# A fused attention and MLP kernel: w_out loaded in 2 KB rows, w_in read in plain slices, and the first tile transposed in fp32

## The chip, the cores and the metric

The kernel runs on one core of a Trainium2 chip. The metric is the device time of one execution in microseconds; the kernel before takes 257.83 us (median of 3 runs, 257.62 to 258.07).

The engines are called PE (TensorE: matmuls and transposes), ACT (ScalarE: exp, tanh, copies), DVE (VectorE), POOL (GpSimd) and SP (SyncE, which only issues DMAs here). PEld is the loading of PE's stationary operand, which runs beside the matmuls. SPq and POOLq are DMA issues of those engines.

## The reference

The computation is an attention over 4 batches of 8 heads, 768 positions, head size 64, followed by an MLP over the 3,072 tokens of 512 features:

```python
scores = q @ k.T / 8                      # per batch and head, 768 x 768
# retrieval heads: causal mask; the others: causal and
# (one of the first 4 keys, or among the last 64 keys)
scores = where(mask, scores, -1e9)
a = softmax(scores)
x = (a @ v), heads laid side by side      # 3072 x 512
h = x @ w_in                              # 512 x 2048
g = h - tanh(h)
out = g @ w_out                           # 2048 x 512
```

Inputs and output are fp32. Which heads are retrieval heads comes as data.

## The kernel before

The tokens are cut into 12 tiles of 256 (three per batch). For each tile the kernel loads q, k and v in fp32, casts them to fp16, transposes q and k, computes scores, exp, the product with v, transposes the result x, and runs the MLP on it: `ph` = w_in times x, `th` = tanh, `gt` = ph - tanh, `po` = gt times w_out. In tiles 0 to 2 PE transposes q and k (`st_T`); in later tiles the heads are sorted by rank, and the DMA engines transpose.

No engine's program is written in order. Operations are collected with a duration, their reads and writes; a list scheduler, run while the program is built, plays them through and emits them in the order of its clock. So a changed duration can move instructions anywhere:

```python
class Plan:
    def op(self, eng, ns, fn, r=(), w=(), dma=None, prio=None, port=False, after=None): ...
    def run(self):
        ...                                   # the earliest operation that is ready goes next
        if dma:
            packets, each = dma               # packets, ns of each on one of 16 DMA engines
            rings["POOL" if e == "POOL" else "SP"].append(
                [i, t + ns + (1200 if e == "POOL" else 300), each, packets * each / 16]
            )
        ...
        for i in order:
            self.ops[i][2]()
```

Tokens are loaded by SP, a block of 128 positions at a time. A row of one head is 256 bytes:

```python
op("SP", max(420, 128 * nh * 1.1),
   lambda: nc.sync.dma_start(
       out=r()[:, i, h0 : h0 + nh, :],
       in_=src[b, h0 : h0 + nh, s0 : s0 + 128, :].rearrange("h p d -> p h d")),
   w=[("raw", idx, i, x) ...], dma=(128 * nh, 18.3), after=after)
```

The weights are loaded by POOL, which casts them to fp16 on the way. Each w_out load brings 512 rows. Partition p takes four rows that follow each other in memory, 8 KB in one piece:

```python
def load_w_out(j, w_after):
    w = lazy(w_pool, [128, 4, DM], FP16, f"wout{j}", f"wout{j}")
    op("POOL", 900,
       lambda: nc.gpsimd.dma_start(
           out=w()[:].rearrange("p i m -> p (i m)"),
           in_=moe_w_out[j * 512 : (j + 1) * 512, :].rearrange("(p i) m -> p (i m)", p=128)),
       r=w_after, w=[("wout", j)], dma=(512, 77.0))
```

With that layout, row 4p + i of w_out stands in slot i of partition p. So `H_unit` has to produce the features of a block in that order, and takes every fourth column of w_in as the stationary operand:

```python
for cb in range(HP):
    nc.tensor.matmul(
        out=ph()[:, j, :], lhsT=w()[:, cb, c0 + fb % 4 : c0 + 512 : 4],
        rhs=xTs[t]()[:, cb, :], start=(cb == 0), stop=(cb == HP - 1))
```

The first tile is cast by ACT and DVE, and then transposed like tiles 1 and 2:

```python
cast_qk(0, (("ACT", "ACT"), ("ACT", "DVE")), (0,))
load(1, halves=range(2))
for n in (0, 1):                          # n counts pairs of heads
    st_T(n, "ACT", ("DVE", "DVE"))
    for f in scores(n): f()
cast_v(0, ("POOL", "POOL"), (0,))
cast_qk(0, (("ACT", "ACT"), ("ACT", "DVE")), (1,))
...

def st_T(n, eq="DVE", ek=("DVE", "DVE")):
    tp, key = bank([128, 2, 8, 128], FP16, "sc", f"tp{n}")
    ...
    nc.tensor.transpose(out=o, in_=t16s[nm, t]()[:, i, 2*hp : 2*hp+2, :], identity=ident16[:])
    ...                                   # eq copies q out of PSUM, ek[0] and ek[1] copy k
```

The product with v of a pair of heads (`av`) reads the cast values `v`, and for keys far from the query `vf`, a copy scaled by the head's flag.

Of the kernel before, what the change touches and what calls it, by code (L numbers as in the profile page):

```python
# [7 lines left out]
FP32 = mybir.dt.float32  # L8
FP16 = mybir.dt.float16
# [3 lines left out]
TT = 256  # L13
# [136 lines left out]
def kernel(  # L150
# [63 lines left out]
    ones = const.tile([128, 128], FP16, name="ones")  # L214
    warm = const.tile([128, 1], FP32, name="warm")
    ident16 = const.tile([128, 128], FP16, name="ident16")
    A4 = const.tile([128, 4, 128], FP16, name="A4")
    sinks = const.tile([128, 128], FP16, name="sinks")
    nz = const.tile([128, 2 * H], FP32, name="nz")
# [29 lines left out]
    def program(first):  # L249
# [27 lines left out]

        raws = {}

        def paired(nm, t):  # L280

            return nm != "v" and t < 0

        def load(t, names="qkv", halves=(None,), blocks=range(NB), after=None):

            b, g = divmod(t, NG)
            for half in halves:
                h0, nh = (0, H) if half is None else (half * HH, HH)
                for nm in names:
                    src = {"q": q, "k": k, "v": v}[nm]  # L290
                    if (nm, t) not in raws:
                        idx = rot["raw"] = rot.get("raw", -1) + 1
                        raws[nm, t] = (
                            lazy(raw_pool, [128, NB, H, D], FP32, "raw", f"raw_{nm}{t}"), idx
                        )
                    r, idx = raws[nm, t]
                    if paired(nm, t):
                        if blocks[0]:
                            continue
                        op(  # L300
                            "SP", max(420, 128 * nh * 1.1),
                            lambda r=r, src=src, h0=h0, nh=nh: nc.sync.dma_start(
                                out=r()[:].rearrange("p i h d -> p (i h d)").rearrange(
                                    "p (h c) -> p h c", h=H
                                )[:, h0 : h0 + nh, :],
                                in_=src[b, h0 : h0 + nh, g * TT : (g + 1) * TT, :].rearrange(
                                    "h (p e) d -> p h (e d)", e=NB
                                ),
                            ),
                            w=[  # L310
                                ("raw", idx, i, x)
                                for i in range(NB) for x in (range(2) if half is None else (half,))
                            ],
                            dma=(128 * nh, 26.0), after=after,
                        )
                        continue
                    for i in blocks:
                        s0 = g * TT + i * 128
                        op(
                            "SP", max(420, 128 * nh * 1.1),  # L320
                            lambda r=r, i=i, src=src, s0=s0, h0=h0, nh=nh: nc.sync.dma_start(
                                out=r()[:, i, h0 : h0 + nh, :],
                                in_=src[b, h0 : h0 + nh, s0 : s0 + 128, :].rearrange("h p d -> p h d"),
                            ),
                            w=[("raw", idx, i, x) for x in (range(2) if half is None else (half,))],
                            dma=(128 * nh, 18.3), after=after,
                        )

        W_IN = ((0, 512), (512, 512), (1024, 512), (1536, 512))

        def load_w_in(c0, n, w_after):
            w = lazy(w_pool, [128, HP, n], FP16, f"win{c0}", f"win{c0}")
            op(
                "POOL", 900,
                lambda: nc.gpsimd.dma_start(
                    out=w()[:],
                    in_=moe_w_in[:, c0 : c0 + n].rearrange("(cb p) f -> p cb f", p=128),
                ),  # L340
                r=w_after, w=[("win", j) for j in range(c0 // 512, (c0 + n) // 512)],
                dma=(512 * n // 512, {512: 85.0, 1024: 80.0, 2048: 77.0}[n]),
            )
            for j in range(c0, c0 + n, 512):
                w_in_t.append((w, j - c0))

        def load_w_out(j, w_after):
            w = lazy(w_pool, [128, 4, DM], FP16, f"wout{j}", f"wout{j}")
            op(
                "POOL", 900,  # L350
                lambda: nc.gpsimd.dma_start(
                    out=w()[:].rearrange("p i m -> p (i m)"),
                    in_=moe_w_out[j * 512 : (j + 1) * 512, :].rearrange("(p i) m -> p (i m)", p=128),
                ),
                r=w_after, w=[("wout", j)], dma=(512, 77.0),
            )
            w_out_t.append(w)

# [23 lines left out]
        if first:  # L382
# [27 lines left out]
                )  # L410


            select(ident16[:], ones[:], 0.0, 0, 1, -1, "ident", ALU.is_equal)
            select(A4[:, 2, :], ones[:], 0.5, window_i - 1, -1, 1, "A4")
            select(sinks[:], ones[:], 0.5, n_sink_i - 1, 0, -1, "sinks")
# [195 lines left out]
        def t16_keys(nm, t, half):  # L611
            return [("t16q", t, half) if nm == "q" else ("k16", t % 2, half)]

        def cast_qk(t, engines, halves=range(2)):

            for half in halves:
                for nm, es in zip("qk", engines):
                    if (nm, t) not in t16s:
                        t16s[nm, t] = tokens(nm, t)
                    c = t16s[nm, t]  # L620
                    r, slot = raws[nm, t]
                    hs = slice(half * HH, half * HH + HH)
                    cast_op(
                        es[half], NB * HH * D,
                        lambda nm=nm, c=c, hs=hs: (
                            c()[:, :, hs, :].rearrange("p i h d -> p h i d") if paired(nm, t)
                            else c()[:, :, hs, :]
                        ),
                        lambda nm=nm, r=r, hs=hs: (
                            r()[:].rearrange("p i h d -> p (i h d)").rearrange(  # L630
                                "p (h i d) -> p h i d", h=H, i=NB
                            )[:, hs, :, :] if paired(nm, t) else r()[:, :, hs, :]
                        ),
                        r=[("raw", slot, i, half) for i in range(NB)], w=t16_keys(nm, t, half),
                    )

# [181 lines left out]
        def st_T(n, eq="DVE", ek=("DVE", "DVE")):  # L818
            t, hp = divmod(n, HP)
            b, g = divmod(t, NG)  # L820
            tp, key = bank([128, 2, 8, 128], FP16, "sc", f"tp{n}")
            keys = [(*key, x) for x in range(2)]
            if hp == 0:
                qT[t] = lazy(qt_pool, [128, HP, TT], FP16, "qT", f"qT{t}")

            def turn(x, nm):
                for i in range(NB):
                    o = tp()[:, x, i, :]
                    if paired(nm, t):
                        o = tp()[:, x, 0:NB, :].rearrange("p i c -> p (i c)")[:, i : NB * 128 : NB]  # L830
                    nc.tensor.transpose(
                        out=o, in_=t16s[nm, t]()[:, i, 2 * hp : 2 * hp + 2, :], identity=ident16[:],
                    )

            for x, nm in enumerate("qk"):
                op(
                    "PE", 112, lambda x=x, nm=nm: turn(x, nm),
                    r=t16_keys(nm, t, hp * 2 // HP) + ["ident"], w=keys[x : x + 1],
                )

            cost = {"ACT": 373, "DVE": 288}
            kk = kz[b % 2][:, 2 * hp : 2 * hp + 2, :]
            op(
                eq, cost[eq],
# [289 lines left out]
        def H_unit(t, u):  # L1134
# [3 lines left out]
            for j in range(FU):  # L1138

                def mm(j=j):  # L1140
                    fb = u * FU + j
                    w, c0 = w_in_t[fb // 4]
                    for cb in range(HP):
                        nc.tensor.matmul(  # L1144
                            out=ph()[:, j, :], lhsT=w()[:, cb, c0 + fb % 4 : c0 + 512 : 4],
                            rhs=xTs[t]()[:, cb, :], start=(cb == 0), stop=(cb == HP - 1),
                        )

                op(
                    "PE", 4 * 109, mm,  # L1150
                    r=[("win", u * FU // 4)] + x_keys(t), w=[key],
                )
# [106 lines left out]

        for b in range(2):  # L1260
            ones_v(b)
        cast_qk(0, (("ACT", "ACT"), ("ACT", "DVE")), (0,))
        load(1, halves=range(2))
        for n in (0, 1):
            st_T(n, "ACT", ("DVE", "DVE"))
            for f in scores(n):
                f()
        cast_v(0, ("POOL", "POOL"), (0,))
        cast_qk(0, (("ACT", "ACT"), ("ACT", "DVE")), (1,))
        for n in (0, 1):  # L1270
            st_A(n, 0)
            st_A(n, 1)
# [10 lines left out]
            cast_qk(1, (("ACT", "ACT"), ("ACT", "ACT")), (half,))  # L1283
            cast_v(1, ("POOL", "POOL"), (half,))
        if first:
            for c0, n in W_IN:
                load_w_in(c0, n, [("v1", 0, 1, 0)])
        load(2)
        scale_v(0, "POOL")
        scale_v(1)  # L1290
# [136 lines left out]
```

## Time and profile before

| | |
|---|---|
| time, median of 3 | 257.83 us |
| span of the profiled execution | 256.3 us |
| busy PE / PEld / DVE / ACT / POOL | 231.5 / 176.8 / 145.1 / 147.3 / 96.0 us |
| read from and written to HBM | 27.27 and 6.29 MB |
| matmuls of ph, 768 of 256 columns | 100.1 us, 273 ns each |
| matmuls of po, 368 of 512 columns and 32 of 256 | 99.1 us, 373 ns each |
| loads of w_in slices as stationary operand | 113 ns each |
| w_in and w_out, four loads each, issue to landing | 11.2 and 11.0 us (median) |

The duration of one matmul includes the time in PE's pipeline, so matmuls overlap and the mean says nothing of the pace; the distance between starts does. The duration of a DMA from issue to landing includes its time in the queue. A wait in the profile is put down to what ended last. The digit rows of the page cut the span into 40 slices of 6.4 us; each digit is a share in tenths.

The part up to about 50 us is the start: tokens of the first tiles and both weights come in, and attention runs ahead of the MLP. Behind it PE alternates between attention of a later tile and the MLP of an earlier one.

### The profile page before, as it was taken

The page shows a single profiled execution, that of the slowest core. Times are in us where ns is not written, and L with a number is a line of the kernel's source. Part 1 is how long each engine was busy: PE and PEld are TensorE (multiplying, and loading weights), DVE is VectorE, ACT ScalarE, POOL GpSimd, SP SyncE. Part 2 cuts the span into 40 slices and gives each one's busy share as a digit, 9 for nine tenths or more (in the row PEclk, how much of TensorE's full clock was granted, in tenths as well). Part 3 has the DMA queues.
Part 4 walks back from the last instruction along what each step waited for, and adds up shares of the span by engine and source line. Part 5 has one row for each costly group of instructions (what it writes and reads, how often), then busy time and mean ns, then how long its engine had stood idle before and what let it go on. Part 6 is the DMA issues. An engine that isn't in the chain of part 4 may idle for free. (4 is left out here: it accounts for less than half of the span.)

```text
span 256.3 us, 6128 instructions
## 1 busy us (share of the span) xinstructions
PE 231.5 (90%) x2220; PEld 176.8 (69%) x2220; DVE 145.1 (57%) x359; ACT 147.3 (57%) x229; POOL 96.0 (37%) x288
## 2 busy tenths in 40 slices
PE   1788986697899899999979999999999999999992
PEld 0456965485677678777757777777788777777761
DVE  7556768246357764656746545566767554643410
ACT  3578857277364938655556664755666656444330
POOL 5382610139954733928625168318520000000000
PEclk9999999599999999999999999999999999999999
DMA  6999999995699799979999899699970311031121
GB/s 140 218 213 196 209 225 220 220 210 97 154 180 172 144 168 243 185 193 208 161 209 203 168 206 211 164 158 218 200 164 3 83 43 42 3 82 43 41 82 48
DMA packets 120131, 39.25 MB, mean 153 GB/s; under 512 B 114336, under 2 KB 116640, under 8 KB 120096
## 3 DMA queue, kind: packets, MB, share of 16 engines
q1 hardware_dynamic: 117120, 34.49, 69.1%
q0 software_dynamic: 2688, 4.19, 8.9%
q8 instruction: 18, 0.29, 0.5%
q14 instruction: 17, 0.14, 0.2%
q10 hardware_dynamic: 288, 0.14, 0.2%
HBM read 27.27 MB, written 6.29 MB: 131 GB/s over the span
## 5 line engine op out<-in xcount | busy, mean ns | idle before, releaser
L1144 PE MATMUL ph<-xT,win 128*128 128x256 f16 x768 | 100.1, 273 | 0.4 <-DVE gt L1164 0.3
L1203 PE MATMUL po<-wout,gt 128*128 128x512 f16 (+1 forms) x400 | 99.1, 373 | 0.9 <-ACT ot L1179 0.9
L1164 DVE SCALAR_TENSOR_TENSOR gt<-th,ph 128x512 f16<-128x512 f32 x96 | 65.9, 686 | 52.0 <-ACT th L1157 51.6
L1157 ACT ACTIVATE th<-ph 128x512 f32<-128x512 f32 x96 | 57.5, 599 | 59.1 <-PE ph L1144 58.9
L1144 PEld LDWEIGHTS <-win 128*128 128x128 f16 x768 | 80.9, 113 | 8.0 <-issue 0.6
L990 ACT ACTIVATE pt<-sc 128x768 f16<-128x768 f32 (+1 forms) x60 | 54.1, 917 | 23.1 <-PE sc L972 23.0
L1203 PEld LDWEIGHTS <-gt 128*128 128x128 f16 x400 | 37.0, 98 | 23.5 <-issue 1.7
L972 PE MATMUL sc<-qT,kz 128*128 128x256 f16 (+1 forms) x280 | 34.2, 257 | 2.7 <-DMA qT<-t_q 2.1
L1039 PEld LDWEIGHTS <-pt 128*128 128x128 f16 x552 | 27.2, 99 | 13.1 <-issue 4.5
L972 PEld LDWEIGHTS <-kz 128*128 128x128 f16 x280 | 24.1, 102 | 12.6 <-issue 1.8
L669 POOL CAST k<-raw_k 128x128 f16 x72 | 19.4, 316 | 33.3 <-DMA raw_k<-in_k_dram 28.6
L1039 PE MATMUL av<-v,pt 128*128 128x65 f16 x304 | 26.7, 196 | 4.4 <-POOL v L602 4.4
L669 POOL CAST t_q<-raw_q 128x128 f16 x72 | 19.8, 314 | 14.2 <-DMA raw_q<-in_q_dram 8.8
L669 POOL CAST v<-raw_v 128x128 f16 x72 | 19.3, 319 | 11.0 <-DMA raw_v<-in_v_dram 11.0
L1069 DVE TENSOR_TENSOR x16t<-av,rinv 128x128 f32 x72 | 20.9, 290 | 2.1
L1039 PE MATMUL av<-vf,pt 128*128 128x65 f16 x248 | 20.5, 195 | 0.0
L915 ACT ACTIVATE pt<-sc 128x1024 f16<-128x1024 f32 (+1 forms) x18 | 17.2, 956 | 3.8 <-PE sc L901 3.1
L1008 DVE TENSOR_TENSOR pt<-pt,m 128x1024 f16<-128x1024 f16 x16 | 13.5, 842 | 10.0 <-ACT pt L990 10.0
L1179 ACT ACTIVATE ot<-po 128x512 f32<-128x512 f32 (+1 forms) x24 | 14.2, 593 | 8.5 <-PE po L1203 8.5
L1059 DVE RECIPROCAL rinv<-av 128x4 f32<-128x4 f32 x48 | 8.6, 179 | 17.5 <-PE av L1039 17.4
L932 DVE TENSOR_TENSOR pt<-pt,mS 128x512 f16<-128x512 f16 x24 | 9.7, 444 | 7.9 <-ACT pt L915 7.9
L901 PE MATMUL sc<-qT,kz 128*128 128x128 f16 x132 | 10.3, 219 | 0.3 <-ACT pt L990 0.3
(71 smaller groups left out, 122.8 us busy)
## 6 DMA issues: line engine op xcount, KB each, us to landing
out_dram<-ot SPq DMA_DIRECT2D x23, 256.0 KB, 2.2
raw_q<-in_q_dram SPq DMA_DIRECT2D x20, 256.0 KB, 4.2
raw_k<-in_k_dram SPq DMA_DIRECT2D x20, 256.0 KB, 4.3
raw_v<-in_v_dram SPq DMA_DIRECT2D x20, 256.0 KB, 4.7
win<-in_moe_w_in_dram POOLq DMA_DIRECT2D x4, 512.0 KB, 11.2
wout<-in_moe_w_out_dram POOLq DMA_DIRECT2D x4, 512.0 KB, 11.0
raw_q<-in_q_dram SPq DMA_DIRECT2D x8, 128.0 KB, 3.7
raw_k<-in_k_dram SPq DMA_DIRECT2D x8, 128.0 KB, 3.8
```

Of the source, the lines that this page charges most:

```text
L669: nc.gpsimd.tensor_copy(out=o, in_=r()[:, :, at, :])
L915: lambda: nc.scalar.activation(out=pt()[:, :, 0:wid], in_=sc()[:, :, 0:wid], func=AF.Exp, scale=inv_sqrt_d),
L972: nc.tensor.matmul(out=sc()[:, hh, o : o + nb * 128], lhsT=kk[:, hh, jb * KS : jb * KS + 128], rhs=q_of(t, hp)[:, q0 * 128 : (q0 + nb) * 128],
L990: lambda: nc.scalar.activation(out=pt()[:, :, 512 * gi : 512 * gi + wid], in_=sc()[:, :, 0:wid], func=AF.Exp, scale=inv_sqrt_d,),
L1008: nc.vector.tensor_mul(out=pv, in0=pv, in1=m4[:, hs, 256:512].unsqueeze(2).to_broadcast([128, 2, 2, 256]),)
L1039: nc.tensor.matmul(out=av()[:, i, hh, :], lhsT=pt()[:, hh, co : co + 128], rhs=vv, start=(jb == first_jb), stop=(jb == qb),)
L1069: nc.vector.tensor_mul(out=x16s[t]()[:, :, at, :], in0=av()[:, :, hh : hh + 1, 0:D], in1=rinv()[:, :, hh : hh + 1].unsqueeze(3).to_broadca ...
L1144: nc.tensor.matmul(out=ph()[:, j, :], lhsT=w()[:, cb, c0 + fb % 4 : c0 + 512 : 4], rhs=xTs[t]()[:, cb, :], start=(cb == 0), stop=(cb == HP ...
L1157: lambda: nc.scalar.activation(out=th()[:], in_=ph()[:], func=AF.Tanh, scale=1.0 / XS),
L1164: lambda: nc.vector.scalar_tensor_tensor(out=gts[t]()[:, u * FU : (u + 1) * FU, :], in0=th()[:], scalar=-XS, in1=ph()[:], op0=ALU.mult, op ...
L1179: nc.scalar.activation(out=ot()[:, c0:c1], in_=po()[:, c0:c1], func=AF.Copy, scale=1.0 / XS)
L1203: nc.tensor.matmul(out=po()[:, c0:c1], lhsT=gts[t]()[:, f, ts * 128 : ts * 128 + 128], rhs=w_out_t[f // 4]()[:, f % 4, c0:c1], start=(f == ...
```

## The change

Three things are changed by hand.

- w_out comes in single rows of 2 KB: row p of each group of 128 goes to partition p. That is the plain layout, so the slices of w_in that make the stationary operand are 128 columns that follow each other.
- The first tile's q and k are no longer cast. PE transposes the fp32 values as they were loaded, with an fp32 identity and into an fp32 PSUM tile; the copies out of PSUM give fp16.
- Leftovers go: an unused way to load pairs of positions, and a list of column ranges for w_in.

The durations that the scheduler is told for these operations change with them, so the order on every engine is planned anew. The diff, cut to its core:

```diff
+    ident32 = const.tile([128, 128], FP32, name="ident32")
...
-                lambda: nc.gpsimd.dma_start(
-                    out=w()[:].rearrange("p i m -> p (i m)"),
-                    in_=moe_w_out[j * 512 : (j + 1) * 512, :].rearrange("(p i) m -> p (i m)", p=128),
+                lambda: nc.gpsimd.dma_start(
+                    out=w()[:],
+                    in_=moe_w_out[j * 512 : (j + 1) * 512, :].rearrange("(fb p) m -> p fb m", p=128),
                 ),
-                r=w_after, w=[("wout", j)], dma=(512, 77.0),
+                r=w_after, w=[("wout", j)], dma=(512, 85.0),
...
+            select(ident32[:], ones[:], 0.0, 0, 1, -1, "ident32", ALU.is_equal)
             select(ident16[:], ones[:], 0.0, 0, 1, -1, "ident", ALU.is_equal)
...
-            tp, key = bank([128, 2, 8, 128], FP16, "sc", f"tp{n}")
+            dt, ident, ns = (FP32, ident32, 440) if t == 0 else (FP16, ident16, 112)
+            tp, key = bank([128, 2, 16 // mybir.dt.size(dt), 128], dt, "sc", f"tp{n}")
...
+                if t == 0:
+                    c, slot = raws[nm, t]
+                    r = [("raw", slot, i, hp * 2 // HP) for i in range(NB)] + ["ident32"]
+                else:
+                    c, r = t16s[nm, t], t16_keys(nm, t, hp * 2 // HP) + ["ident"]
+                op("PE", ns, lambda x=x, c=c: turn(x, c), r=r, w=keys[x : x + 1])
...
-            cost = {"ACT": 373, "DVE": 288}
+            cost = {"ACT": 373, "DVE": 420 if t == 0 else 288}
...
-                            out=ph()[:, j, :], lhsT=w()[:, cb, c0 + fb % 4 : c0 + 512 : 4],
+                            out=ph()[:, j, :], lhsT=w_in_t[fb // 4]()[:, cb, f0 : f0 + 128],
...
-        cast_qk(0, (("ACT", "ACT"), ("ACT", "DVE")), (0,))
         load(1, halves=range(2))
...
-        cast_qk(0, (("ACT", "ACT"), ("ACT", "DVE")), (1,))
```

More of the change, by code (lines that the diff above doesn't have):

```diff
@@ L278, in program @@
         raws = {}
-        def paired(nm, t):
-            return nm != "v" and t < 0
         def load(t, names="qkv", halves=(None,), blocks=range(NB), after=None):
@@ L296, in load @@
                     r, idx = raws[nm, t]
[L297 to L316, printed above, removed]
                     for i in blocks:
@@ L327, in load, with load_w_in @@
                         )
-        W_IN = ((0, 512), (512, 512), (1024, 512), (1536, 512))
-        def load_w_in(c0, n, w_after):
-            w = lazy(w_pool, [128, HP, n], FP16, f"win{c0}", f"win{c0}")
+        def load_w_in(j, w_after):
+            w = lazy(w_pool, [128, HP, 512], FP16, f"win{j}", f"win{j}")
             op(
@@ L338, in load_w_in @@
                     out=w()[:],
-                    in_=moe_w_in[:, c0 : c0 + n].rearrange("(cb p) f -> p cb f", p=128),
+                    in_=moe_w_in[:, j * 512 : (j + 1) * 512].rearrange("(cb p) f -> p cb f", p=128),
                 ),
-                r=w_after, w=[("win", j) for j in range(c0 // 512, (c0 + n) // 512)],
-                dma=(512 * n // 512, {512: 85.0, 1024: 80.0, 2048: 77.0}[n]),
-            )
-            for j in range(c0, c0 + n, 512):
-                w_in_t.append((w, j - c0))
+                r=w_after, w=[("win", j)], dma=(512, 85.0),
+            )
+            w_in_t.append(w)
         def load_w_out(j, w_after):
@@ L623, in cast_qk @@
                     cast_op(
[L624 to L633, printed above, removed]
+                        es[half], NB * HH * D, lambda c=c, hs=hs: c()[:, :, hs, :],
+                        lambda r=r, hs=hs: r()[:, :, hs, :],
                         r=[("raw", slot, i, half) for i in range(NB)], w=t16_keys(nm, t, half),
@@ L824, in st_T, with turn @@
                 qT[t] = lazy(qt_pool, [128, HP, TT], FP16, "qT", f"qT{t}")
-            def turn(x, nm):
+            def turn(x, c):
                 for i in range(NB):
-                    o = tp()[:, x, i, :]
-                    if paired(nm, t):
-                        o = tp()[:, x, 0:NB, :].rearrange("p i c -> p (i c)")[:, i : NB * 128 : NB]
                     nc.tensor.transpose(
-                        out=o, in_=t16s[nm, t]()[:, i, 2 * hp : 2 * hp + 2, :], identity=ident16[:],
+                        out=tp()[:, x, i, :], in_=c()[:, i, 2 * hp : 2 * hp + 2, :],
+                        identity=ident[:],
                     )
             for x, nm in enumerate("qk"):
[L836 to L839, printed above, removed]
-            cost = {"ACT": 373, "DVE": 288}
+                if t == 0:
[5 more added lines that the diff above has]
+            cost = {"ACT": 373, "DVE": 420 if t == 0 else 288}
             kk = kz[b % 2][:, 2 * hp : 2 * hp + 2, :]
@@ L1141, in mm @@
                     fb = u * FU + j
-                    w, c0 = w_in_t[fb // 4]
+                    f0 = (fb % 4) * 128
                     for cb in range(HP):
                         nc.tensor.matmul(
-                            out=ph()[:, j, :], lhsT=w()[:, cb, c0 + fb % 4 : c0 + 512 : 4],
+                            out=ph()[:, j, :], lhsT=w_in_t[fb // 4]()[:, cb, f0 : f0 + 128],
                             rhs=xTs[t]()[:, cb, :], start=(cb == 0), stop=(cb == HP - 1),
@@ L1285, in program @@
         if first:
-            for c0, n in W_IN:
-                load_w_in(c0, n, [("v1", 0, 1, 0)])
+            for j in range(4):
+                load_w_in(j, [("v1", 0, 1, 0)])
         load(2)
```

## The prediction

> **What bounds the kernel now.** I read the page's busy times and slices first, then the waits, then the busy times by stage, then the timeline around the one long wait, and last the DMA queues of two stretches.
>
> ```profile
> PE 231.5 (90%) x2220; PEld 176.8 (69%) x2220; DVE 145.1 (57%) x359; ACT 147.3 (57%) x229; POOL 96.0 (37%) x288
> PE   1788986697899899999979999999999999999992
> PEclk9999999599999999999999999999999999999999
> DMA  6999999995699799979999899699970311031121
> ```
>
> TensorE (PE) is busy for 90% of the span, and its lows, the tail apart, are in the first ten slices of 6.4 us. The clock digit falls once, to 5, in the eighth slice (44.9 to 51.3 us). The DMA engines are full from the second slice to the ninth.
>
> A busy PE need not be at its pace, so I take the pace from a steady stretch:
>
> ```profile
> 102.09 1.04 PE L1144 MATMUL ph<-xT,win 128*128 128x256 f16 x8
> 102.96 1.03 PE L1203 MATMUL po<-wout,gt 128*128 128x512 f16 x4
> 103.82 0.38 PE L972 MATMUL sc<-qT,kz 128*128 128x256 f16 x3
> ```
>
> Eight matmuls of 256 columns start 0.87 us before the next group: 109 ns each. Four of 512 columns take 0.86 us: 215 ns each. Both are 2.4 columns per ns plus 2 or 3 ns. By that rate all matmuls are about 220 us of streaming; the other 36 us are lost, and I add them up from the start times: 17 us by 42.4, another 6.5 by 52, about 7 between 52 and 160, hardly any until 250, and the 5 us tail. So 42 to 52 is the stage to look at.
>
> ```profile
> PE av L1039 <- POOL v L602: 4.4, 1, 4.4
> POOL v L602 <- DMA raw_v<-in_v_dram: 16.6, 4, 10.9
> ```
>
> These are the waits (total us, times, longest us). By stage:
>
> ```profile
> 24.00:42.40 18.40, 17.16 (x197) 15.58 (x197) 12.68 (x31) 13.95 (x24) 5.06 (x9) 1.00 1.16 214
> 42.40:47.00 4.60, 0.24 (x7) 0.15 (x6) 2.28 (x13) 0.70 (x2) 0.71 (x2) 0.78 1.03 216
> 47.00:52.00 5.00, 5.00 (x37) 3.46 (x37) 1.95 (x8) 1.73 (x2) 0.47 (x1) 0.52 0.99 214
> 52.00:60.00 8.00, 8.00 (x96) 6.21 (x95) 3.82 (x10) 6.45 (x12) 4.28 (x16) 1.00 0.88 192
> ```
>
> The columns are span, busy time of PE, PEld, DVE, ACT and POOL, clock, DMA share, GB/s. PE stands still for 4.36 us, and then runs 5.0 us at a clock of 0.52, which costs another 5.0 x 0.48 = 2.4 us.
>
> ```profile
> 24.80 8.01 SPq L321 DMA_DIRECT2D raw_v<-in_v_dram  x2
> 29.62 2.25 POOL L351 DMA_DIRECT2D wout<-in_moe_w_out_dram x4
> 46.29 1.18 POOL L602 CAST v<-raw_v 128x512 f16<-128x512 f32 x2 [10.88 <-DMA raw_v<-in_v_dram]
> 46.96 0.22 PE L1039 MATMUL av<-v,pt 128*128 128x65 f16 x1 [4.36 <-POOL v L602]
> ```
>
> PE waits for a cast, the cast for the second block of V of tile 2. The landing times give that block an issue at 29.3 and a landing at 46.17 us, 16.9 us later, where the first block landed at 34.9. What it shared the DMA engines with is w_out, whose four parts landed from 37.6 to 45.6. The queues in 25 to 30 us (while w_in is loaded) and in 36 to 40 us (w_out) show how (packets, MB, share of 16 engines):
>
> ```profile
> q0 software_dynamic: 782, 0.78, 91.9%
> q1 hardware_dynamic: 784, 0.20, 29.9%
> ```
>
> ```profile
> q0 software_dynamic: 211, 0.78, 96.7%
> q1 hardware_dynamic: 205, 0.05, 9.7%
> ```
>
> The weights (q0) and the rows of q, k, v (q1, 256 B each) alternate one packet for one. A round takes 5.0 us x 16 / 782 = 102 ns with w_in's 2 KB rows, and 4.0 us x 16 / 211 = 303 ns with w_out's 8 KB rows. So the layout of w_out sets how fast V arrives.
>
> **What the Trainium skill says.** "DMA: Bandwidth & Descriptors", section "Queues, rings and completion order", says that each DMA engine goes round-robin over the queues it has work for, a packet at a time; the counts 782 to 784 and 211 to 205 agree. "TensorE: Matmul & The Clock Gate", Part 1, says that the clock is halved once an activity window of about 3.4 us passes idle; the 0.52 behind the 4.36 us wait agrees, and the waits of 1.8 and 1.7 us later leave the clock at 1.00. The same page, "Terms", gives the array a transpose mode that is 4 times faster for fp32; no fp32 matmul is in this trace, so I leave open whether the new transposes run in one pass or in four.
>
> **The change part by part.**
>
> 1. *w_out in 2 KB rows.* The block of V is 1,024 rows and 16 closing packets: 65 rounds per DMA engine. Before: w_out has (128 + 16) x 4 / 16 = 36 rounds of 303 ns = 10.9 us, with 36 of the 65 rows in them; the other 29 rows follow at about 15 ns, so some 11.3 us. From 33.1 us (the first block's landing less 1.8) that gives 44.4, plus 1.8 to land = 46.2, as measured. After: 65 rounds of 102 ns = 6.6 us, so a landing at 41.5 to 42, a cast of 0.62 us, and a release of PE at about **42.5** in place of 46.96. w_out itself takes (512 + 16) x 4 / 16 = 132 rounds of 102 ns = 13.5 us in place of 10.9. Its last part lands near 48.2; its first user stands 7.4 us of matmuls behind the wait, at 49.9 or later, so this stays hidden. The tokens behind it (q, k, v of tile 3) land some 1.4 us later.
>
> 2. *Plain stationary slices of w_in.* The loads with a step of four elements take 113 ns, those of scores 102 and of po 98. All lie beside matmuls that start every 109 ns, which is the streaming rate: 0.
>
> 3. *First tile in fp32.* Removed: 3 casts on ScalarE of 0.62 us and one on VectorE of 0.43. Added: one select on GpSimd (0.29), wider copies out of PSUM on VectorE (two per head pair, 0.29 each before; the kernel's own plan has 0.42), and dearer transposes: 16 of them. In one pass they cost what the fp16 ones do. In four passes they are 512 columns in place of 128: 160 ns more each at full clock (2.6 us in all), about 320 at half clock (5.1). In this stage the matmuls of 128 columns start 105 to 110 ns apart, so the clock is the low one until about 14 us. The chain of the first pair gains: its q and k land at 4.8 and 6.0 us, and the first exp starts at 8.9; without the casts I get about 8.1 even in four passes. Later pairs give that back. By the end of tile 0 I take the two as even. From 22 us on PE is paced by w_in, whose four parts land at 22.6, 25.9, 29.3 and 32.7 in both.
>
> 4. *The order.* The instructions are ordered by the kernel's own plan, whose costs changed. In the new PE order the eight matmuls of ph of tile 1, unit 3 stand behind the wait for V, no longer ahead of it: 8 x 109 = 0.87 us of work moves behind. PE then comes to the wait near 41.5, so about 1 us of waiting is left, too short to lower the clock. The scores of tile 4 come 3.2 us of PE work earlier, those of tile 5 1.3, of tile 7 1.5.
>
> The sum: 42.5 - 46.96 = -4.5; the work moved behind +0.9; no half clock -2.4: together **-6.0**. Against it: the transposed q of tile 4 landed at 79.7 and was used at 82.6, 2.9 us of slack for 3.2 (+0.3); that of tile 5 at 96.0 for 96.7 (+0.6); tile 7 already waits 1.7 us and comes 1.5 earlier (up to +1.5). **+2.2** in all. -3.8 from 257.8 gives **254.1 us**.
>
> **The rivals.**
>
> - *The start becomes the bound.* If the fp32 transposes take four passes at half clock and their 5.1 us fall on the chain of the head pairs, PE comes to the wait at 44 to 45 instead of 41.5. For it: the chain from transpose to exp is serial there. Against it: w_in paces PE from 22.6 to 33, and the casts leave the chain. Time: 256 to 257.
> - *The gain is given back in tiles 3 to 7.* Loads are tied to PE's progress, but a DMA engine full from 90 to 110 us (share 1.08 and 1.21) may not be able to run 5 us earlier. For it: tile 7's wait on a DMA transpose. Against it: the DMA digits of 5, 6 and 7 between 58 and 115 us, room of several us. Time: 256.5 to 258.
> - *V does not come earlier*, because the share goes by bytes and not by packets. Then w_out's longer stay only costs: about 259. The packet counts speak against it.
> - *More comes of it*: a start earlier by a microsecond and none of the later waits growing: 251.5 to 252.5.
>
> **Range and chances.** The gain at the wait is the surest part (5 to 6 us); what of it survives to the end is not. I put the middle at 254.1, and the range from 251.6 (nearly all kept) to 257.4 (start or middle eats nearly all). Faster by over 2% means under 252.7: 0.23. Slower by over 2% means over 263, which needs a new wait of 5 us on top of no gain: 0.03. Within 2%: 0.74.
>
> **What would show it.** In the new profile: q0 and q1 one for one at about 102 ns a round until about 47 us; V's second block landing near 42; PE's wait for the cast of v at 1 us or less, and no digit of 5 in the clock row; the last w_out landing near 48 with no wait of po on it; the first exp near 8 us; matmul pace of ph still 109 ns. It would be wrong if fp32 transposes of 400 ns or more show PE arriving late at the wait, if the clock falls elsewhere, or if waits on transposed q in tiles 4 to 7 add up to more than about 4 us.

## The result and the profile after

The kernel after takes **0.9848** of the time of the kernel before (95% interval 0.982 to 0.9877): 253.7 and 253.9 us against a median of 257.73 us. Two further timed runs of it, at 257.7 and 259.0 us, were disturbed and are not in the ratio. That is within 2%, and 254.1 us was predicted. The total is right by luck; two of the terms behind it are not, and they nearly cancel.

The page of the kernel after, the busy times first, then the rows of the slices:

```profile
PE 230.2 (91%) x2220; PEld 167.6 (67%) x2220; DVE 144.2 (57%) x358; ACT 144.8 (57%) x226; POOL 97.7 (39%) x289
...
PE   2888986899999899999899899998999999999992
...
PEclk9999999999999999999999999999999999999999
DMA  6999999999899999898999979499960311031111
```

A slice is 6.3 us here. The 5 in the clock row is gone. Of PE's lows around the wait a 6 stays in the seventh slice (37.8 to 44.1 us); single 8s follow in the slices that start at 44, 63, 101, 120, 139 and 170 us. PE's waits (total us, times, longest us):

```profile
PE av L1005 <- POOL v L574: 2.8, 1, 2.8
PE ph L1110 <- DMA xT<-x16t: 2.6, 3, 1.4
```

The wait for V has shrunk from 4.4 to 2.8 us, not to the 1 us that was computed. A new entry stands behind it: PE waits 2.6 us, in three pieces, for transposed x. By stage (span, busy PE, PEld, DVE, ACT, POOL, clock, DMA share, GB/s):

```profile
41.98:44.76 2.78, 0.00 (x1) 0.00 (x0) 1.33 (x11) 0.45 (x1) 0.67 (x2) 1.00 1.23 198
44.76:52.00 7.24, 7.16 (x94) 5.73 (x94) 4.99 (x17) 5.01 (x8) 2.72 (x9) 1.00 1.04 216
```

PE stands still for 2.78 us and goes on at full clock. The timeline around it (start, us, engine, line, operation):

```profile
24.81 8.01 SPq L298 DMA_DIRECT2D raw_v<-in_v_dram  x2
30.32 3.04 POOL L322 DMA_DIRECT2D wout<-in_moe_w_out_dram  x4
44.09 1.18 POOL L574 CAST v<-raw_v 128x512 f16<-128x512 f32 x2 [8.64 <-DMA raw_v<-in_v_dram]
44.76 0.19 PE L1005 MATMUL av<-v,pt 128*128 128x65 f16 x1 [2.78 <-POOL v L574]
```

The V block landed at 43.97 us, where 41.5 to 42 was computed and 46.17 was measured before. The DMA queues tell why. First 34.5 to 36 us, then 40 to 44 us (packets, MB, share of 16 engines):

```profile
q0 software_dynamic: 298, 0.30, 122.3%
q1 hardware_dynamic: 3, 0.00, 0.2%
```

```profile
q0 software_dynamic: 629, 0.63, 92.0%
q1 hardware_dynamic: 625, 0.16, 29.7%
```

In the second stretch the queues alternate one for one, 4.0 x 16 / 629 = 102 ns a round, as computed. In the first the queue of the token rows has three packets in 1.5 us: the block was issued at 29.3, but its packets began only at 36.0 and were at their pace from 36.2. 36.2 plus 65 rounds of 102 ns is 42.9, and the landing came 1.1 us behind.

For all kernels I add up PE's lost time as the prediction did for the kernel before: distance between starts, less columns / 2.4 ns and 2.5 ns. An fp32 transpose counts as 128 columns, so its longer run is in the loss.

| profiled run | wait for V, us | lost by 60 us | lost from 60 to 180 us | lost from 75 to 180 us | waits for DMA in 75 to 180 us | ratio to before |
|---|---|---|---|---|---|---|
| before | 4.4 | 23.7 | 6.6 | 3.9 | 2.1 | 1 |
| after | 2.8 | 20.3 | 6.0 | 5.2 | 3.4 | 0.985 |
| before, 2 KB rows (e1) | 2.1 | 19.0 | 6.8 | 5.9 | 3.8 | 0.990 |
| after, fp16 tile (e8) | 2.4 | 19.0 | 7.1 | 6.5 | 4.2 | 0.989 |
| after, told of V (e5) | 0 | 19.5 | 8.0 | 6.8 | 4.7 | 0.985 |
| before, told of V (e6) | 0 | 17.9 | 8.4 | 8.0 | 4.6 | 0.979 |
| after, V on a second queue (e7) | 0 | 18.2 | 9.1 | 7.4 | 5.6 | 0.993 |
| fp16 tile, told of V (e11) | 0 | 17.7 | 7.5 | 7.4 | 5.5 | 0.987 |
| fp16 tile, told of V and xT (e9) | 0 | 17.9 | 2.8 | 2.7 | none listed | 0.974 |
| before, told of V and xT (e10) | 0 | 17.9 | 3.6 | 3.6 | none listed | 0.976 |
| after, told of V and xT (e12) | 0 | 18.4 | 3.1 | 1.7 | none listed | 0.970 |

The names in brackets are those of the experiments below. The losses are of one profiled execution each, and the ratios come from the timed runs. The profiled execution of e5 took 255.3 us where its four runs span 251.7 to 255.3, that of e6 253.9 where they span 251.0 to 253.9. From 75 to 180 us the first eight kernels lose what they wait for DMA and about 2 us more; e6 has another 1.7 for a halved clock.

### The profile page after: what moved, and what is told of

It reads as the page before. It is cut to its first block, busy times and chain, and to the rows that moved or that the text cites. A ratio compares the mean times of both kernels' runs of the same rounds, so it can differ in the third digit from the quotient of the medians.

```text
span 252.0 us, 6126 instructions
## 1 busy us (share of the span) xinstructions
PE 230.2 (91%) x2220; PEld 167.6 (67%) x2220; DVE 144.2 (57%) x358; ACT 144.8 (57%) x226; POOL 97.7 (39%) x289
## 5 line engine op out<-in xcount | busy, mean ns | idle before, releaser
L1169 PE MATMUL po<-wout,gt 128*128 128x512 f16 (+1 forms) x400 | 98.1, 370 | 1.2 <-ACT ot L1145 1.2
L1110 PEld LDWEIGHTS <-win 128*128 128x128 f16 x768 | 71.4, 98 | 18.6 <-DMA xT<-x16t 3.8
L1005 PEld LDWEIGHTS <-pt 128*128 128x128 f16 x552 | 26.8, 98 | 14.7 <-issue 4.7
L938 PEld LDWEIGHTS <-kz 128*128 128x128 f16 x280 | 23.2, 98 | 11.0 <-DVE kz L780 3.9
L633 POOL CAST t_q<-raw_q 128x128 f16 x72 | 20.3, 317 | 18.4 <-DMA raw_q<-in_q_dram 17.4
L974 DVE TENSOR_TENSOR pt<-pt,m 128x1024 f16<-128x1024 f16 x16 | 11.4, 710 | 8.0 <-ACT pt L956 8.0
```

The costliest lines, as they stand in the source:

```text
L633: nc.gpsimd.tensor_copy(out=o, in_=r()[:, :, at, :])
L938: nc.tensor.matmul(out=sc()[:, hh, o : o + nb * 128], lhsT=kk[:, hh, jb * KS : jb * KS + 128], rhs=q_of(t, hp)[:, q0 * 128 : (q0 + nb) * 128],
L974: nc.vector.tensor_mul(out=pv, in0=pv, in1=m4[:, hs, 256:512].unsqueeze(2).to_broadcast([128, 2, 2, 256]),)
L1005: nc.tensor.matmul(out=av()[:, i, hh, :], lhsT=pt()[:, hh, co : co + 128], rhs=vv, start=(jb == first_jb), stop=(jb == qb),)
L1110: nc.tensor.matmul(out=ph()[:, j, :], lhsT=w_in_t[fb // 4]()[:, cb, f0 : f0 + 128], rhs=xTs[t]()[:, cb, :], start=(cb == 0), stop=(cb == H ...
L1169: nc.tensor.matmul(out=po()[:, c0:c1], lhsT=gts[t]()[:, f, ts * 128 : ts * 128 + 128], rhs=w_out_t[f // 4]()[:, f % 4, c0:c1], start=(f == ...
```

## The experiments

The first four ran beside a kernel before of 257.81 us, the second four beside 256.81, the third three beside 256.41, the last beside 256.92; so ratios are compared, not microseconds.

**e1: only the layout.** The kernel before, its order kept, with w_out in 2 KB rows. The rows of w_out sit in other slots than the features that meet them, so another product is computed; the work is the same.

```diff
-                    out=w()[:].rearrange("p i m -> p (i m)"),
-                    in_=moe_w_out[j * 512 : (j + 1) * 512, :].rearrange("(p i) m -> p (i m)", p=128),
+                    out=w()[:],
+                    in_=moe_w_out[j * 512 : (j + 1) * 512, :].rearrange("(fb p) m -> p fb m", p=128),
```

> The kernel before with w_out loaded in 2 KB rows and nothing else; every engine keeps its order. Theory A (the packet share of w_out sets when V of tile 2 arrives, and that is the gain): V's second block lands near 44.0 instead of 46.2 us, PE is released near 44.8 and has waited 2.3 us instead of 4.4, the clock does not fall, time 253.0 to 254.0 us. Rival B (the gain is the fp32 first tile or the new order): V may land earlier, but the time stays at 257 to 258 us. Rival C (the plain stationary slices of w_in): also 257 to 258, as the slices keep their step of four here.

Measured: 0.990 (0.9871 to 0.9929). V landed at 43.79 us and PE's wait was

```profile
PE av L1039 <- POOL v L602: 2.1, 1, 2.1
```

with the clock at 1.00. The layout alone takes 4.7 us off the lost time by 60 us, and about two thirds of the time that the whole change brings (1.0% of 1.5%, with intervals that overlap a little).

**e2: the change without the layout.** The kernel after with 8 KB rows, the diff of e1 backwards; again another product.

> The changed kernel with w_out in 8 KB rows again, order kept, plain slices kept. Theory A: V's second block lands at 46.2 us, PE waits about 5 us from 42.0, the clock falls to a half for some 4 to 5 us, time 258.0 to 258.8 us. Rivals B and C (fp32 tile, order or plain slices carry the gain): 253.5 to 254.5 us.

Measured: 1.0184 (1.0125 to 1.0243), so slower than before.

```profile
PE av L1005 <- POOL v L574: 4.9, 1, 4.9
```

V landed at 46.37 us, and the clock was half from 44.3 to 51.1. With e1 this settles that the rows of w_out set when V lands. It is slower than was expected, too. The order of the kernel after comes to the wait earlier with less work done, which costs 0.8 us by 60 us; and a wait of 2.56 us for xT at 123.4 halved the clock again, from 126.2 to 129.7, about 1.7 us more.

**e3: only the fp32 tile.** The kernel before with the first tile transposed in fp32 and planned anew; 8 KB rows and stepped slices stay.

```diff
+            dt, ident, ns = (FP32, ident32, 440) if t == 0 else (FP16, ident16, 112)
...
-        cast_qk(0, (("ACT", "ACT"), ("ACT", "DVE")), (0,))
-        cast_qk(0, (("ACT", "ACT"), ("ACT", "DVE")), (1,))
```

> The kernel before with the first tile transposed in fp32 and not cast, planned anew; w_out in 8 KB rows and the stepped slices of w_in as before. Theory A: worth nothing, because PE then waits for V at 46.2 us anyway: 257.3 to 258.5 us, with a wait of 4 to 5 us and one fall of the clock. Rival B: 253.5 to 255 us.

Measured: 0.9982 (0.9958 to 1.0007). The wait was 4.2 us and the clock fell from 48.3 to 51.7. With V late, the fp32 tile and the order that comes with it bring nothing. The new order isn't neutral: it issued the V block at 31.3 us in place of 29.3, and V landed at 47.83.

**e4: the wait without the halved clock.** The kernel before, with the first four products of the ninth pair repeated 16 times ahead of the wait, about 2 us of extra work; the last pass gives the result.

```diff
-                    for jb in range(first_jb, qb + 1):
+                    again = 16 if n == 8 and i == 0 and hh == 0 else 0
+                    for x, jb in [(0, j) for j in range(4)] * again + [
+                        (1, j) for j in range(first_jb, qb + 1)
+                    ]:
```

> The kernel before; the first four matmuls of the product with v on which PE then waits are done 16 times more, 64 matmuls of 65 columns, about 1.9 us of work ahead of the wait, with no use. V arrives as before (PE released at 46.9 to 47.0 us); the wait is 2.4 to 2.6 us instead of 4.4. If the half clock behind the wait is a cost of its own, made by the length of the idle time: the clock stays at 1.00 and the time falls by 2.0 to 2.4 us to 255.3 to 255.7 us. If the clock fell for another reason or costs nothing: 257.5 to 258 us.

Measured: 1.0206 (1.0113 to 1.0299), a miss. The wait was 2.66 us, and the clock fell all the same, from 47.1 to 50.5, and again from 125.6 to 129.0 behind a wait of 2.78 us for xT. These are the two lows of its clock row:

```profile
PEclk9999999799999999999899999999999999999999
```

It doesn't separate wait and clock. What it shows is that a wait of this length may or may not cost the clock: 2.78 us in the kernel after did not. The last section works out which does.

**e5: the same kernel, told when V comes.** In the kernel after the plan believes that the V block lands at 38.3 us. One number changes, and with it only the order: 3.2 us more PE work stands ahead of the wait.

```diff
-                            dma=(128 * nh, 18.3), after=after,
+                            dma=(1750 if (nm, t, i) == ("v", 2, 1) else 128 * nh, 18.3), after=after,
```

> The kernel after, with one number of the kernel's own plan changed: the second block of V of tile 2 counts as 1,750 packets in place of 1,024, so that the plan no longer believes it lands at 38.3 us. Nothing but the order of instructions changes; by the instruction order 28.75 us of matmuls stand ahead of the first product with that V, against 25.58. Theory A (what is left of the gain is the 2.8 us wait that the late V leaves, and PE has other work to put there): PE comes to the wait about 3.2 us later, near 45, the wait is 0 to 0.4 us, the clock stays at 1.00 and the whole takes 2 to 2.8 us less than the kernel after: about 249.5 us of span, 251 to 251.8 us of time, a ratio of 0.973 to 0.978 to the kernel before. Rival B (the gain is given back later, by the transposed q of tiles 4 to 7): the wait goes and waits of 1 us or more appear between 80 and 180 us, the time stays at 253 to 254. Rival C (the work that is moved ahead is itself not ready, tanh or w_out missing): lost time by 60 us stays at 20 us.

Measured: 0.9846 (0.9777 to 0.9916), no different from the kernel after. The wait for V is gone, but waits for xT and qT between 75 and 180 us grew from 3.4 to 4.7 us. Rival C of the expectation holds in part as well: of the 2.8 us of waiting that went, only 0.8 is left by 60 us (20.3 to 19.5), as PE lost more ahead of that, 1.1 us of it in a wait for w_in (0.3 in the kernel after). My theory that only the wait was left fell; the interval would still hide a gain of 0.7%.

**e6: the same number in the kernel before** (2,100 packets; 8 KB rows and fp16 stay).

> The kernel before, 8 KB rows of w_out and fp16 first tile kept, with the same number of the plan set to 2,100 packets: 30.94 us of matmuls ahead of the first product with the late V, against 25.60. V still lands near 46.2 us. Theory A (the layout matters only through the wait, so order alone can hide it): PE comes to the wait at 47 to 48, the wait is under 0.5 us, no fall of the clock, lost time by 60 us falls from 23.7 to 18 or 19 us, time 251.5 to 253.5, a ratio of 0.975 to 0.983. Rival (the work is not ready ahead of V, since w_out lands from 37.6 to 45.6 and tanh and gate lag): the wait shrinks but others of 1 to 2 us come in, time 255 to 257.

Measured: 0.9794 (0.9732 to 0.9857). V landed as late as ever and nobody waited for it: lost time by 60 us fell to 17.9. But in the stretch from 75 to 180 us PE's waits are now led by

```profile
PE ph L1144 <- DMA xT<-x16t: 4.6, 2, 3.0
```

and its longest, 2.97 us at 117.9, halved the clock from 121.1 to 124.5. The layout isn't needed to hide V; the order does it as well, and the gain is partly given back.

**e7: V on a second queue.** The kernel after, the V block issued by ScalarE at 28.2 us instead of SyncE, so that it has a DMA queue of its own.

```diff
-                            "SP", max(420, 128 * nh * 1.1),
+                            "ACT" if (nm, t, i) == ("v", 2, 1) else "SP",
...
+                            r=[("win", 2)] if (nm, t, i) == ("v", 2, 1) else (),
```

> The kernel after, but the second block of V of tile 2 is issued by ScalarE, at the same place in time (about 29.3 us), so that it has a DMA queue of its own beside that of the other q, k, v rows. Theory A (the stretch from 34.5 to 36.2 us in which the queue of the token rows is empty belongs to that queue, which had not taken in the block's descriptors): its packets begin by 32 us, share the engines with two queues until the first block is in, and it lands between 39 and 41 in place of 43.97; PE, which comes at about 42, does not wait, and the time is 2 to 2.8 us under that of the kernel after: 251 to 252, ratio 0.974 to 0.979. Rival B (it is not the queue but what the engines can do with 256-byte rows beside w_out): a landing of 43 to 44.5 and the time of the kernel after, 253.7 to 254. Possible cost in both: ScalarE is held by the issue of 1,024 rows for about 1.2 us near 29.3.

The queues between 32 and 34 us, q10 being the new one:

```profile
q10 hardware_dynamic: 986, 0.25, 68.4%
q1 hardware_dynamic: 890, 0.22, 62.9%
q0 software_dynamic: 8, 0.01, 1.9%
```

Its packets went out four us earlier than in the kernel after, in a stretch in which w_out had not begun, and the block landed at 35.3 us, 7.1 us after its issue and earlier than I had expected. From 34.5 to 36 us the token queue sent 210 packets beside 246 of w_out. So the empty stretch was a matter of the token queue, not of the engines or of w_out. PE no longer waited for V. And yet: 0.9929 (0.9902 to 0.9956), less gain than with the wait. PE's longest total is now

```profile
PE ph L1114 <- DMA xT<-x16t: 4.7, 3, 2.5
```

It lost 9.1 us between 60 and 180, 3.1 more than the kernel after. V 8.7 us earlier brought no time. (The plan has one queue more here and orders a few other instructions differently too.)

**e8: the kernel after with the fp16 tile.** The diff of e3 backwards, in the kernel after.

> The kernel after with one part undone: the first tile's q and k are cast and transposed in fp16 as before; 2 KB rows of w_out, plain slices of w_in and the plan's cost of w_out stay. Work ahead of the late V as in the kernel before, 25.6 us. Theory A (the fp32 tile brings nothing of its own, 0.998 with an interval over 1 when it was tried on the kernel before): V lands near 43.9, PE waits 2 to 2.5 us, clock at 1.00, time 253.5 to 255, ratio 0.984 to 0.990, as the kernel before with 2 KB rows (0.990). Rival B (the fp32 tile or the order that it brings carries part of the gain in the kernel after): ratio 0.990 or more and at least 1 us slower than 253.8. Rival C (the fp32 tile costs, by its two passes at half clock): ratio under 0.983.

Measured: 0.9889 (0.9813 to 0.9964), not to be told from the kernel after or from e1; V landed as early, and PE waited 2.4 us. Theory A stands: in this order the fp32 tile brings nothing that these intervals can show.

**e9, e10, e11: told of xT as well.** If PE comes too early to the matmuls ph of some tiles because the plan believes that xT lands earlier than it does, a second number mends it. (The expectations call them tiles 4 and 5. Counted from 0, with 64 matmuls of ph to a tile, the waits stand ahead of tiles 3, 5 and, in some runs, 8.) e9 is e8 with both numbers, e10 the kernel before with both, e11 e8 with the V number alone.

```diff
-                    r=[("x16t", t)], w=[("xT", t, "all", i)], dma=(512, 22.0),
+                    r=[("x16t", t)], w=[("xT", t, "all", i)], dma=(512, 66.0),
```

> The kernel after with the fp16 first tile, and two numbers of the plan changed: the late V block counts as 1,750 packets, and a packet of the transposes of x to xT counts as 66 ns in place of 22, so that the plan no longer believes xT lands as early. By the instruction order the first matmul of ph of tile 5 stands behind 100.2 us of PE work in place of 96.4, that of tile 4 behind 81.2 in place of 78.9. Theory A (what is won at the wait for V is given back where PE comes too early to ph of tiles 4 and 5, because xT lands near 84.5 and 121 whatever happened before): these waits, 1 to 3 us in the variants with the least loss by 60 us, fall under 0.5 us; lost time by 60 us stays 18 to 19 us and by 160 us is 22 to 24 us in place of 26; time 249 to 251 us, ratio 0.970 to 0.978. Rival (the DMA engines are the bound of the stretch from 60 to 140 us, so the waits only move to other transposes): the waits for DMA between 75 and 180 us add up to 4 us or more again, time 252.5 to 254.

> The kernel before, with its 8 KB rows of w_out and its fp16 tile, and the same two numbers of the plan: 2,100 packets for the late V block, 66 ns for a packet of xT. Nothing but order changes. Theory A: the 3.0 us wait for xT of tile 5 that the version with only the V number had falls under 0.5 us, lost time by 60 us near 18 us and by 160 us 22 to 24; time 249 to 251, ratio 0.970 to 0.978, so that the layout of w_out is worth nothing once the order is right. Rival (DMA bound): 252.5 to 254 again with waits on other transposes.

> The kernel after with the fp16 first tile and only the V number of the plan changed (1,750 packets). It separates the two numbers. Theory A: no wait for V, lost time by 60 us about 17 us, and then a wait of 2 to 3 us for xT near 119 and others, so lost time by 160 us is 25.5 to 26.5 us, as with all the others; time 252.5 to 254, ratio 0.980 to 0.988. Rival (nothing is given back): lost time by 160 us is 24 us, time 250 to 251.

Measured: e9 **0.9738** (0.971 to 0.9766), e10 **0.9756** (0.9724 to 0.9788), e11 0.9872 (0.9827 to 0.9918). The page of e9:

```profile
PE 229.9 (93%) x2220; PEld 167.1 (68%) x2220; DVE 145.0 (59%) x359; ACT 147.1 (59%) x229; POOL 98.4 (40%) x289
...
PE   1788989999999999999999999999999999989992
...
PEclk9999999999999999999999999999999999999999
```

From the seventh slice to the thirty-fifth every digit of PE is a 9, where the kernel after has the 6 and six 8s. No wait of PE for a DMA between 75 and 180 us is in e9's or e10's list. e11, which differs from e9 in the xT number alone and is slower by 1.3%, has there

```profile
PE ph L1110 <- DMA xT<-x16t: 3.3, 2, 1.9
```

The DMA engines are no bound of that stretch, then: the same bytes went through the same queues in another order. That order moved both sides. PE comes to ph of tile 3 at 86.9 us in e9 and at 83.8 in e11, for an xT that lands at 85.4 and 85.2; it comes to ph of tile 5 at 120.5 and 117.4, for an xT that lands at 117.5 and 119.3.

**e12: the kernel after with both numbers**, fp32 tile and all.

> The kernel after as it is, fp32 first tile and all, with the two numbers of the plan (1,750 packets for the late V block, 66 ns for a packet of xT). It differs from the version with 0.9738 in the first tile alone, with nothing behind it left to swallow or to hide a difference. Theory A (fp32 transposes in two passes at half clock and the later start of ph make the first tile 1 to 1.5 us dearer than with casts): lost time by 30 us is 15.5 to 16.3 us in place of 14.75, the time is 250.3 to 251.2 us, ratio 0.978 to 0.981. Rival B (even, as I took it in the prediction): ratio 0.972 to 0.976, lost time by 30 us near 14.8. Waits for xT between 75 and 180 us under 0.5 us in both.

Measured: 0.9702 (0.967 to 0.9734), a median of 249.68 us. It lost 15.4 us by 30, against 14.7 in e9, but its time isn't above e9's 249.48; theory A missed. e9, e10 and e12 all beat both kernels. Their intervals overlap, and e12 ran apart from the others, so none of the three is shown to be the best.

## Why the prediction was right, and where its steps were not

- **w_out in 2 KB rows.** The mechanism held: a round of 102 ns, the last part of w_out at 48.16 (48.2 was computed), nobody waiting for it. "DMA: Bandwidth & Descriptors", section "Queues, rings and completion order", gives the turns by packet, and 629 to 625 agrees. The mis-sized term is the start. I let the packets of the second block follow the first at 33.1 us; they began at 36.0. PE was released at 44.76 in place of 42.5, and the landing came 2.2 us earlier than before, half of what was computed. The trace of before could have told: its queue of token rows is as empty from 34.5 to 36 us, with one packet in it. There the block's 1,040 packets went out from 36.0 to 44.3 us, so in 8.3 us and not in 11.3 from 33.1, because some 150 packets of w_out had gone out ahead of them. That my sum for the kernel before met the measured 46.2 was two errors that cancelled.
- **Plain slices.** Loads of w_in took 98 ns instead of 113, and ph kept its 273 ns. No run took this part alone, but e8 and e1 differ only in it, in the plan's cost of w_out with the order that follows, and in one unused mask, with 0.989 and 0.990; it is worth nothing that shows, as computed.
- **fp32 tile.** The question of one pass or four has a third answer. At half clock the transposes start 213 ns apart, two each of q and k from 8.81 us; at full clock 110:

```profile
8.81 0.64 PE L794 MATMUL tp<-ident,raw_q 128*128 128x128 f32 x2
9.23 0.63 PE L794 MATMUL tp<-ident,raw_k 128*128 128x128 f32 x2
...
14.01 0.39 PE L794 MATMUL tp<-ident,raw_q 128*128 128x128 f32 x2
14.23 0.38 PE L794 MATMUL tp<-ident,raw_k 128*128 128x128 f32 x2
```

  That is twice the time of the fp16 ones (107 and 56 ns), as two passes would take. The first exp came at 9.05 us, not 8.1 (8.92 before), as VectorE was busy with the masks when the first k was to be copied. "Even by the end of tile 0" held: 13.7 us lost by 20 us in both kernels.
- **The order and the clock.** PE came to the wait at 41.98 (41.5 was computed), and the clock stayed up. That it stayed up was luck: the wait was 2.8 us and not 1, and it lay across two of the clock's windows (last section). Waits of 2.66 us in e4 and of 2.56 in e2 cost the clock.
- **The sum at the wait.** -6.0 was computed, -3.4 measured by 60 us (23.7 to 20.3). Term by term it is -2.2 for the release in place of -4.5, +0.9 for the work moved behind and -2.4 for the clock, together -3.7. (From 42.4 to 52 us the kernel before loses 6.9 us, not 6.5: 4.4 of waiting and 2.5 of half clock.)
- **What is given back.** +2.2 was computed, for the transposed q of tiles 4, 5 and 7. From 75 to 180 us +1.3 was measured (3.9 to 5.2), and not through q: PE's waits for q fell from 2.1 to 0.8 us, and 2.6 us of waiting for x of tiles 3, 5 and 8 came in, which I had not seen. Where the loss by 60 us fell by 5.5 us or more without a change to the xT number (e6, e7, e11), 3.5 to 4.1 us came back in that stretch.
- **A term that I had passed over.** The kernel before loses 2.7 us between 60 and 75 us, the kernel after 0.8. The difference is one wait, behind a slow operation of VectorE:

```profile
60.97 2.99 DVE L1008 TENSOR_TENSOR pt<-pt,m 128x1024 f16<-128x1024 f16 x1
64.35 0.28 PE L1117 MATMUL xp<-ident,x 128*128 128x128 f16 x2 [1.80 <-DVE x L1083]
```

  The mean of that operation is 0.84 us; why this one took 2.99 isn't shown. No other run has the wait. In the rows of the kernel before it is the 7 and the 8 in PE's tenth and eleventh slices, and there is another 7 in the twenty-first; I had written that the lows end with the tenth.

So -3.8 was computed as -6.0 + 2.2. The spans of the profiled executions fell by 4.3 us: -3.4 by 60 us, -2.0 to 75, +1.3 to 180 and -0.2 behind. That the totals agree is luck: the gain at the wait was little more than half of the one computed, and a wait that nobody had named went away. Of the rivals, "the gain is given back" is the one that bounds this kernel once V is in time: e5, e7, and e11 beside e8 show no gain from removing the rest of the wait, and e9 to e12 that the order of the work, not the DMA engines, is what gives it back.

Left open: what the token queue did between 33 and 36 us (e7 shows only that another queue does not do it); whether moving xT's number also mended the waits for qT directly or by the shift of all that follows; and how much of the 2.5 us that the halved clock cost the kernel before would have reached the end, which e4 was to measure.

## What to carry to other kernels

When the time hardly moves though a long wait shrinks, add up lost time before and behind the wait in one table: here part of what was won at 45 us came back at 86, 121 and 175 us. Where a planner orders the instructions, compare its landing times with those of the trace; mending two of its numbers was worth 2.4% in the kernel before, the better layout 1.0%, and not a byte less was moved. And when a transfer's end is worked out from packet rates, look up in the trace when its first packet goes out.

## What the runs showed of the hardware that I had not expected

- fp32 transposes of 128 x 128 take twice as long as fp16 ones: 213 ns at half clock and about 110 at full, beside 107 and 56.
- A transfer that was issued at 29.3 us on the queue of the other token rows sent its packets from 36.0; on ScalarE's queue, issued at 28.2, they were nearly all out by 34. "DMA: Bandwidth & Descriptors", section "Issuing engines are not separate DMA queues", has a second issuing engine save only the time to initiate. Here it moved the landing from 43.97 to 35.3 us, so in this case the measurement says more.
- "TensorE: Matmul & The Clock Gate", Part 1, halves the clock after an idle window of about 3.4 us, free-running. The traces agree with the window, but it need not be idle throughout. In each of the 14 traces the recorded clock changes, up to the fall at the end of the kernel, only at whole steps of 3.413 us from its first rise; in e4 it does so at 16.34, 47.06, 50.47, 125.56 and 128.98 us, 9, 1, 22 and 1 steps apart. I laid this grid over PE's idle time:

| wait, from | length, us | idle share of its most idle window | clock |
|---|---|---|---|
| e7, 119.4 us | 2.54 | 43% | full |
| e2, 123.4 us | 2.56 | 75% | half from 126.2 |
| e4, 44.8 us | 2.66 | 65% | half from 47.1 |
| after, 42.0 us | 2.78 | 54% | full |
| e4, 122.0 us | 2.78 | 76% | half from 125.6 |
| e6, 117.9 us | 2.97 | 87% | half from 121.1 |

  In all 14 traces the full clock stayed after every window that was idle for 58% or less, and fell at the end of every one that was idle for 60% or more. The wait of the kernel after was split, 28% in one window and 54% in the next. So the edge lies in the idle share of a window, not in the length of a wait. By these figures, as an estimate, a wait of 2.05 us (60% of 3.41) is enough if it falls into one window.
